# A gated mix of two sequence layers on one Trainium2 core: the order of work inside a chunk of the long convolution, its PSUM ring and its table set-up rearranged

## The chip, the cores and the metric

The kernel runs on one core of a Trainium2 chip (trn2). The metric is device time in microseconds; before the change the median of three runs is 465.64 us (462.01 to 466.97). A separate execution was profiled; it took 465.26 us, and the profile covers a span of 463.5 us of it.

Names of engines, as the profile has them: PE is the matrix engine (PEld its weight loads, which overlap), DVE the vector engine, ACT the scalar engine, POOL and SP the engines that here mostly issue DMAs. A name with a q (SPq, POOLq) is the queue from which an engine issues DMAs. PSUM is the memory that PE writes its sums into, and ACT or DVE must empty a PSUM buffer ("evict" it) before PE can use it again.

## The reference

Two layers read the same `x` (2048 x 1024, bf16) and are mixed by a gate. `A` is a diagonal complex state space layer, `B` a short and a long convolution:

```python
g = sigmoid((x * gate_w).sum(-1, keepdims=True))
# A: h[t] = Lam_bar * h[t-1] + (x @ B_bar.T)[t];  a = 2 Re(h @ C.T) + x * Dskip
# B: a filter of 4 taps on k, times v, then a causal convolution over all 2048 steps
k_shift = sum(k_pad[:, t:t+S] * shift_k[:, ks-1-t] for t in range(4))
kv = k_shift * v
y  = irfft(rfft(kv, 4096) * rfft(ssm_k, 4096))[:2048]     # one filter for each of 1024 channels
b  = x * (y + kv * ssm_D)
return g * a + (1 - g) * b
```

## The kernel before

The kernel has two stages. **The convolution stage** does layer B in eight chunks `c` of 128 channels, roughly the first 255 us. **The scan stage** does layer A after that, with the last of B's results brought in from a scratch buffer in DRAM.

The transform of a chunk is done with matrix products against tables of sines and cosines. The 2048 steps are four blocks of 512; each block is folded about its middle (into a part that is even and one that is odd), transformed to four groups of 128 frequencies, multiplied, and transformed back. The steps of a chunk, with the tile names by which the profile shows them:

- `load` (SP): `kT` (k transposed by the DMA), `kn` (the long filter, transposed) and `v`; three buffers in all.
- `dgs` then `taps`: ACT makes four diagonal matrices `dg` from the identity and the short filter; PE multiplies `kT` by them, 64 matmuls of 128 columns into two PSUM buffers `taps`; ACT evicts them to `ks`.
- `times_v`: DVE multiplies `ks` by `v`; PE reverses the lower half (`mirror`, 2 matmuls); ACT evicts that to `lo`; DVE forms `ev` = `ks` - `lo`, and POOL issues a DMA that adds `lo` into `ks`. A `yield` after the product and one after `lo` let the caller place these three pieces apart.
- `fold_K`: PE folds `kn` (`foldk`, 10 matmuls into two buffers); ACT evicts to `eok`.
- `fwd_K(c, hf)`, `fwd_V(c, hf)`: for half `hf` of the frequencies, PE makes `psk` (16 matmuls) and `psv` (8), two PSUM buffers each; ACT evicts them to `Kh` and `Vh`.
- `products(c, hf)`: DVE multiplies `Kh` by `Vh` block by block and sums into `G`; one of the sums is done by a DMA that POOL issues (`G<-t`, accumulating).
- `inverse(c)`: PE makes `psz` from `G` and the tables `CI`, `SI` (2 x 16 matmuls); ACT evicts to `cv`; SP moves it to DRAM.
- `turn_table(pi)`: not part of B. ACT and DVE make one eighth of the rotation tables `TC`, `TS`, `TCi`, `TSi` of the scan stage (`hr`, `TCS`, `m`, `TCSi`); POOL issues a DMA that adds `m`.

**What sets the order.** All compute goes through the helper `put` (line 99, which is why almost every row of the profile names L99). It ties each instruction to the one before it on the same engine, so on every engine instructions run in the order of the Python code. The generators are advanced by `step` (to the next `yield`) and `run` (to the end), and the loop `for c in range(NC)` is a schedule written out by hand. An iteration `c` handles three chunks at once: with `n = c + 1` and `nn = c + 2`, it makes the transforms of `n`, the products of `c`, the inverse of `c - 1` and the taps and the fold of `nn`. On PE the order of an iteration is

```
psk(n,0)  mirror(n)  psz(c-1)  taps(nn)  psv(n,0)  psk(n,1)  foldk(nn)  psv(n,1)
```

and on ACT `hr`, `Kh` x2, `lo`, `cv` x2, `dg` x4, `ks` x2, `hr`, `TCS` x2, `Vh` x2, `Kh` x2, `eok` x2, `m` x2, `Vh` x2, `TCSi`. In the last two iterations there are no more taps and folds; then `Bu` (`bu`, matmuls of layer A) fills in.

PSUM has room for eight units of 2 KB per partition. Before, the pool `psum` has three buffers of two units, taken in turn by everything above, and `psum1` two single units (`p1`, `p2`) for small things: the columns of parameters at the start, the gate, and the last of the four output tiles at the end.

**The start** (before the loop): the tables `CF`, `SF` of the forward transform and `CI`, `SI` of the inverse are computed from indices (`reduced`, `sincos`, `inverse_angles`, `inverse_table`), the parameters are brought to columns by small matmuls (`psp`), and `state_params` works out the constants of layer A. Chunk 0 takes its own way (`first_times_v`).

**The scan stage**: `Bu(tb, g)` gives 2 x 16 matmuls `bu` for each of 4 blocks of time and 4 groups of states, ACT evicts to `U`, DVE does `scan` (two products and sums, the recurrence as a scan instruction `W`, and again two products and sums, to `hb`), and `Cy` gives 32 matmuls `psy` of each output tile from `hb` and `CT`.

Of the kernel before, what the change touches and what calls it, by code (L numbers as in the profile page):

```python
# [20 lines left out]
def kernel(  # L21
# [57 lines left out]
    psum = pool("psum", 3, space=bass.MemoryType.PSUM)  # L79
    psum1 = pool("psum1", 1, space=bass.MemoryType.PSUM)  # L80
# [9 lines left out]

    def ps1(tag):
        return psum1.tile([128, 512], F32, name=tag, tag=tag)
# [52 lines left out]
    tab_pool = h3pool(h3, "tab", 1)  # L145
    ld = h3pool(h3r, "ld", 3, side="right")
# [11 lines left out]
    prow = rows_[64:96, 0:128]  # L158

    nc.scalar.dma_start(out=skr, in_=B_shift_k.rearrange("(j p) k -> j p k", p=128))  # L160
    pih = consts.tile([128, 1], F32, name="pih")
# [3 lines left out]
    put("act", nc.scalar.activation, out=one, in_=pih, func=ACT.Sin)  # L165
    for i, ap in enumerate((A_Lambda_re, A_Lambda_im, A_log_dt, gate_w)):
        nc.scalar.dma_start(out=prow[i * 8:(i + 1) * 8, :], in_=ap.rearrange("(j p) -> j p", p=128))
# [60 lines left out]
    def sincos(rq, n, sin_out, cos_out, sin_scale):  # L228

        fa = u4([128, n], F32, "fa")  # L230
        act(fa, rq, func=ACT.Abs)
        act(sin_out, rq, func=ACT.Sin, scale=sin_scale)
        act(cos_out, fa, func=ACT.Sin, bias=pih, scale=-TWO_PI)
# [27 lines left out]
    pcol = consts.tile([128, 4 + KS, ND], F32, name="pcol")  # L261
    gwb = consts.tile([128, ND], BF16, name="gwb")
    psp = ps1("p1")[:, 0:32 + ND * KS]
    raise_clock(3)
    for k in range(KS):
        mm(psp[:, 32 + ND * k:32 + ND * (k + 1)], skr[:, :, k], ident[32:32 + ND, 32:32 + ND], True, True)
    raise_clock(6)

    def dgs(c, on_dve=False):
        dg = ks_pool.tile([128, KS, 128], BF16, name="dg", bufs=1)  # L270
        for k in range(KS):
            if on_dve:
                ts(dg[:, k], ident, pcol[:, 4 + k, c:c + 1], None, ALU.mult)
            else:
                act(dg[:, k], ident, func=ACT.Identity, scale=pcol[:, 4 + k, c:c + 1])
        return dg

    hf = u4([128, 2, 512], F32, "h")
    for mt in range(2):
        ts(hf[:, mt], fr_, colm[:, mt:mt + 1], None, ALU.mult)  # L280
    copy(pcol[:, 4:], psp[:, 32:].rearrange("p (i j) -> p i j", j=ND))
# [11 lines left out]
    def inverse_angles(h2):  # L293

        if h2 == 0:
            inv["room"] = xt_pool.tile([128, 2, 2, 512], F32, name="h", tag="xT")
        hi = inv["room"][:, h2]
        for k in range(2):
            fi = 2 * h2 + k
            ts(hi[:, k], trow[0], inv["col"][:, fi:fi + 1], inv["at0"][:, fi:fi + 1], ALU.mult, ALU.add)  # L300
        rq = w4([128, 1024], F32, "rq")
        ts(rq, flat(hi), MAGIC, -MAGIC, ALU.add, ALU.add)
        tt(flat(hi), flat(hi), rq, ALU.subtract)
        return flat(hi)

    def inverse_table(h2, rq):
        sincos(rq, 1024, flat(SI[:, 2 * h2:2 * h2 + 2]), flat(CI[:, 2 * h2:2 * h2 + 2]), -TWO_PI)


    Lre, Lim, logdt = pcol[:, 0], pcol[:, 1], pcol[:, 2]  # L310
# [12 lines left out]
    def state_params():  # L323

        mm(psp[:, 0:32], prow, ident[64:96, 64:96], True, True)
        copy(pcol[:, 0:4], psp[:, 0:32].rearrange("p (i j) -> p i j", j=ND))
        copy(gwb, psp[:, 24:32])
        yield
        dtv = small("dtv")
        act(dtv, logdt, func=ACT.Exp)  # L330
        av = small("av")
        tt(av, dtv, Lre, ALU.mult)
        bv = small("bv")
        tt(bv, dtv, Lim, ALU.mult)
        act(rv, av, func=ACT.Exp)
        ts(thn, bv, 1.0 / TWO_PI, None, ALU.mult)
        yield
        thU = small("thU")
        ts(thU, thn, float(TB), None, ALU.mult)
        frs = []  # L340
        for x, name in ((thn, "th"), (thU, "thU")):
            rq = small(name + "_rq")
            ts(rq, x, MAGIC, -MAGIC, ALU.add, ALU.add)
            fr = small(name + "_fr")
            tt(fr, x, rq, ALU.subtract)
            frs.append(fr)
        sc = []
        for fr, name in zip(frs, ("th", "thU")):
            fa = small(name + "_fa")
            act(fa, fr, func=ACT.Abs)  # L350
            s_ = small(name + "_sin")
            act(s_, fr, func=ACT.Sin, scale=TWO_PI)
            c_ = small(name + "_cos")
            act(c_, fa, func=ACT.Sin, bias=pih, scale=-TWO_PI)
            sc += [s_, c_]
        sth, cth, cs["sU"], cs["cU"] = sc
        yield
        rc = small("rc")
        tt(rc, rv, cth, ALU.mult)
        rs = small("rs")  # L360
        tt(rs, rv, sth, ALU.mult)
        nre = small("nre")
        ts(nre, rc, -1.0, None, ALU.add)
        den = small("den")
        tt(den, Lre, Lre, ALU.mult)
        den2 = small("den2")
        tt(den2, Lim, Lim, ALU.mult)
        tt(den, den, den2, ALU.add)
        invden = small("invden")
        put("dve", V.reciprocal, invden, den)  # L370
        ts(invden, invden, 2.0, None, ALU.mult)
        t_a = small("t_a")
        t_b = small("t_b")
        tt(t_a, nre, Lre, ALU.mult)
        tt(t_b, rs, Lim, ALU.mult)
        tt(t_a, t_a, t_b, ALU.add)
        tt(c2r, t_a, invden, ALU.mult)
        tt(t_a, rs, Lre, ALU.mult)
        tt(t_b, nre, Lim, ALU.mult)
        tt(t_a, t_a, t_b, ALU.subtract)  # L380
        tt(c2i, t_a, invden, ALU.mult)
        ts(mc2i, c2i, -1.0, None, ALU.mult)

    def turn_table(pi, home):
# [6 lines left out]
        ts(rq, h, MAGIC, -MAGIC, ALU.add, ALU.add)  # L391
        tt(rq, h, rq, ALU.subtract)
# [5 lines left out]
        m = home([128, 2, TB], BF16, "m")  # L398
# [121 lines left out]
    def products(c, hf, home=u4):  # L520
# [16 lines left out]
        mult(0, 0, t=at(0))  # L537
        n1 = mult(1, 0, home)
        gather(at(1), n1)
        t2 = mult(0, 1, home)  # L540
# [6 lines left out]
        n1 = mult(2, 0)  # L547
        tt(t2[:, :, 3:], t2[:, :, 3:], n2, ALU.add)
        n3 = mult(3, 0)
# [3 lines left out]
        tt(at(2), at(2), n1, ALU.add)  # L553
        tt(g[:, 0], g[:, 0], t2[:, 1], ALU.subtract)
# [28 lines left out]
    def gate(tb):  # L583
        psg = ps1(f"p{1 + tb % 2}")[:, 0:4]
# [157 lines left out]

    none = iter(())
    dg0 = dgs(0)
    act(flat(SF), rqf, func=ACT.Sin, scale=TWO_PI)
    act(flat(hf), rqf, func=ACT.Abs)
    act(flat(CF), flat(hf), func=ACT.Sin, bias=pih, scale=-TWO_PI)
    act(NSF, SF[:, :, 256:512], func=ACT.Copy, scale=-1.0)
    act(NCF, CF[:, :, 0:256], func=ACT.Copy, scale=-1.0)

    trow[0] = consts.tile([128, TB], mybir.dt.float16, name="row")
    copy(trow[0], iota_i32([128, TB], [[1, TB]], 0, 0, "row"))
    inverse_cols()
    rqi = [inverse_angles(0)]
    sp = state_params()
    first = first_times_v(0, dg0)
    step(first)
    step(sp)
    step(first)
    step(sp)  # L760
    fold = fold_K(0)
    step(fold)
    run(first)
    run(fold)
# [4 lines left out]
    fwd_V(0, 0)  # L769
    fwd_K(0, 0)  # L770
    rqi.append(inverse_angles(1))
    taps(1, dg1)
    p0 = products(0, 0)
    step(p0)
# [3 lines left out]
    fwd_V(0, 1)  # L778
    step(tv)
    run(fold_K(1))  # L780

    for c in range(NC):
        n, nn = c + 1, c + 2
        if n == NC:
            break
        if nn < NC:
            load("kT", nn)
            load("kn", nn)
        if c < 4:
            load_BT(c // 2, c % 2)  # L790
        elif c < 6:
            load_xT(0, halves=(c - 4,))
        else:
            load_xT(1)
            load_BT(2, 0)
            load_BT(2, 1)
        tabs = turn_table(c - 1, u4) if c else none
        back = inverse(c - 1) if c else none
        if c:
            tv = times_v(n)  # L800
            step(tv)
            run(p1)
            step(tabs)
            p0 = products(c, 0)
            step(p0)
        p1 = products(c, 1)
        if nn < NC:
            load("v", nn)

        fwd_K(n, 0)  # L810
        if c:
            step(tv)
            run(tv)
            step(p0)
        else:
            step(p0)
            run(tv)
        run(back)
        if nn < NC:
            dg = dgs(nn)  # L820
        step(tabs)
        step(p1)
# [3 lines left out]
        step(tabs)  # L826
        if c == 0:
            step(sp)
            inverse_table(0, rqi[0])
        fwd_V(n, 0)  # L830
# [3 lines left out]
        fwd_K(n, 1)  # L834
        if nn < NC:
            run(fold_K(nn))
        step(tabs)
        if c == 0:
            inverse_table(1, rqi[1])
        fwd_V(n, 1)  # L840
        run(tabs)
# [3 lines left out]
    with tc.tile_pool(name="fin", bufs=1, side="right") as fin:  # L845
# [11 lines left out]
        run(p1)  # L857
        step(ta)
        step(tb_)
        step(p0)  # L860
        step(ta)
        step(tb_)
        run(back)
# [3 lines left out]
        step(p0)  # L867
        Bu(0, 0)
        step(tb_)
        step(tb_)  # L870
        run(tb_)
        p1 = products(c, 1, room)
        step(p1)
# [63 lines left out]
    for tl in range(3):  # L937
        ps = ps2([128, 2, 512], "psy")
        pss.append(([ps[:, 0], ps[:, 1]], [(slice(0, D), flat(ps))]))
    pa, pb = ps1("p1"), ps1("p2")  # L940
    pss.append(([pa, pb], [(slice(0, 512), pa), (slice(512, D), pb)]))
# [44 lines left out]
```

## Time and profile before

| | us | share of the span |
|---|---|---|
| median of three runs | 465.64 | |
| profiled execution | 465.26 | |
| its span | 463.5 | |
| DVE busy | 404.8 | 87% |
| ACT busy | 255.4 | 55% |
| POOL busy | 61.5 | 13% |
| matmuls `psz`, both tables | 99.6 (256 of them) | |
| matmuls `taps` | 34.5 (512) | |
| DVE idle until `lo` is there | 32.2 (6 times) | |
| DVE idle until the DMA `G<-t` has landed | 6.4 (twice) | |
| DMA `G<-t`, median from issue to landing | 5.4 (4.8 to 9.6) | |

Times in a row of the timeline are: start, duration (of all instructions of the row together), engine, line, operation, output<-inputs, shapes, count, and in brackets the idle time of the engine just before and what ended it. Matmul ends are modelled: a single matmul of 512 columns shows 0.38 us, while in an unbroken row the next one starts 0.2157 us later. So the starts are what to read for how long PE really needs.

### The profile page before, as it was taken

How to read it: one execution, taken by the hardware profiler on the slowest of the kernel's cores; microseconds unless marked ns; L12 is line 12 of the kernel's file. 1: busy time of each engine (PE TensorE's matmuls, PEld its weight loads, DVE VectorE, ACT ScalarE, POOL GpSimd, SP SyncE). 2: the span in 40 equal slices, each digit the busy share in tenths (PEclk: the TensorE clock that was granted, in tenths of full speed). 3: DMA queues.
4: the chain of work that ended last, by engine and by line, in shares of the span. 5: the costliest groups of instructions: out<-in, count | busy, mean ns of one | idle time of the engine just before them, and what ended most of it. 6: DMA issues, size and time to landing. Idle time of an engine off the chain costs nothing.

```text
span 463.5 us, 6282 instructions
## 1 busy us (share of the span) xinstructions
PE 423.8 (91%) x2414; PEld 207.1 (45%) x2414; DVE 404.8 (87%) x571; ACT 255.4 (55%) x311; POOL 61.5 (13%) x80
## 2 busy tenths in 40 slices
PE   7986879888897988985999999999999999999995
PEld 4534335453543536442444454444444444444442
DVE  9798459697896969779968999999999999999973
ACT  7677767859496784957462342523443324557201
POOL 3020101211202121021120000011101011032200
PEclk9999799999999998998899999999999999999999
DMA  8597915957669599968331999224495475379513
GB/s 159 116 181 139 171 45 103 195 114 153 140 133 185 103 190 165 125 134 161 81 63 40 186 184 214 53 45 110 99 197 117 114 163 125 77 164 197 116 24 114
DMA packets 134352, 60.20 MB, mean 130 GB/s; under 512 B 118441, under 2 KB 122545, under 8 KB 134322
## 3 DMA queue, kind: packets, MB, share of 16 engines
q1 hardware_dynamic: 123696, 42.22, 41.1%
q0 software_dynamic: 10544, 17.57, 23.4%
q8 instruction: 19, 0.31, 0.3%
q14 instruction: 11, 0.09, 0.1%
q10 hardware_dynamic: 82, 0.02, 0.0%
HBM read 12.86 MB, written 8.39 MB: 46 GB/s over the span
## 4 chain that ended last, share of the span: by engine, by line
PE 71%; ACT 16%; DVE 7%; issue 5%; POOL 0%; DVEq 0%; ACTq 0%; POOLq 0%
PE bu L99 24%; PE psy L99 21%; PE psz L99 11%; PE taps L99 6%; PE psk L99 4%; ACT Vh L99 4%; PE foldk L99 3%; DVE t L99 3%; ACT Kh L99 2%; ACT dg L99 2%; PE p L99 1%; ACT hr L99 1%; ACT TCS L99 1%; ACT cv L99 1%; ACT m L99 1%
## 5 line engine op out<-in xcount | busy, mean ns | idle before, releaser
L99 PE MATMUL bu<-xT,BT 128*128 128x512 bf16 x512 | 112.3, 379 | 0.0
L99 PE MATMUL psy<-CT,hb 128*128 128x512 bf16 x480 | 105.7, 379 | 0.0
L99 DVE TENSOR_TENSOR t<-Kh,Vh 128x1536 bf16<-128x1536 bf16 (+3 forms) x112 | 82.4, 759 | 0.0
L99 PEld LDWEIGHTS <-BT 128*128 128x128 bf16 x512 | 50.0, 98 | 60.2
L99 PEld LDWEIGHTS <-hb 128*128 128x128 bf16 x512 | 50.0, 98 | 59.9
L99 ACT ACTIVATE U<-bu 128x1024 bf16<-128x1024 f32 x32 | 32.7, 1022 | 52.8 <-PE bu L99 50.4
L99 PE MATMUL psz<-G,CI 128*128 128x512 bf16 x128 | 49.9, 390 | 11.7 <-ACT Kh L99 7.2
L99 DVE TENSOR_TENSOR_SCAN W<-rv,init,A 128x512 bf16<-128x512 f32 x48 | 57.7, 1262 | 0.0
L99 PE MATMUL psz<-G,SI 128*128 128x512 bf16 x128 | 49.7, 389 | 0.0
L99 PE MATMUL taps<-dg,kT 128*128 128x128 bf16 x512 | 34.5, 224 | 9.7 <-ACT dg L99 8.4
L99 DVE TENSOR_TENSOR t<-t 128x1536 bf16<-128x1536 bf16 (+1 forms) x64 | 39.6, 618 | 0.5
L99 PEld LDWEIGHTS <-kT 128*128 128x128 bf16 x512 | 31.6, 101 | 14.7 <-issue 13.7
L99 ACT ACTIVATE cv<-psz 128x1024 bf16<-128x1024 f32 x16 | 16.4, 1023 | 39.1 <-PE psz L99 39.1
L99 DVE TENSOR_TENSOR G<-G,t 128x1024 bf16<-128x1024 bf16 x48 | 31.7, 687 | 7.0 <-DMA G<-t 6.4
L99 PE MATMUL psk<-eok,CF 128*128 128x512 bf16 (+1 forms) x96 | 27.6, 370 | 9.7 <-ACT Vh L99 8.8
L99 ACT ACTIVATE Kh<-psk 128x1024 bf16<-128x1024 f32 x32 | 31.7, 1026 | 5.4 <-PE psk L99 5.4
L99 ACT ACTIVATE ga<-psy,gcols 128x1024 bf16<-128x1024 f32 x8 | 8.9, 1113 | 46.3 <-PE psy L99 46.3
L99 DVE TENSOR_TENSOR ev<-ks,lo 128x1024 bf16<-128x1024 bf16 x7 | 4.8, 691 | 32.2 <-ACT lo L99 32.2
L99 ACT ACTIVATE Vh<-psv 128x1024 bf16<-128x1024 f32 x32 | 30.8, 1014 | 0.9 <-PE psv L99 0.9
L99 POOL DMA_DIRECT2D G<-t x16 | 21.2, 1326 | 71.9 <-DVE t L99 63.4
L99 POOL DMA_DIRECT2D pbb<-gd x12 | 10.3, 860 | 133.3 <-ACT gd L99 68.4
L99 PEld LDWEIGHTS <-CF 128*128 128x128 bf16 x160 | 14.9, 98 | 25.2 <-issue 11.8
(139 smaller groups left out, 593.5 us busy)
## 6 DMA issues: line engine op xcount, KB each, us to landing
G<-t POOLq DMA_DIRECT2D x16, 384.0 KB, 5.4
v<-in_B_v_dram SPq DMA_DIRECT2D x8, 512.0 KB, 5.1
cv_scr<-cv SPq DMA_DIRECT2D x16, 256.0 KB, 2.3
pbb<-cv_scr SPq DMA_DIRECT2D x12, 256.0 KB, 3.2
xr<-in_A_x_dram SPq DMA_DIRECT2D x12, 256.0 KB, 3.5
pbb<-gd POOLq DMA_DIRECT2D x12, 256.0 KB, 3.3
TCSi<-m POOLq DMA_DIRECT2D x8, 256.0 KB, 4.0
ga<-xr POOLq DMA_DIRECT2D x8, 256.0 KB, 3.4
```

The lines of the kernel that those rows point to most:

```text
L99: i = f(*a, **kw)
```

## The change

The parts, with the code cut to its core. One ring of PSUM: four buffers of two units, and everything that used `p1` or `p2` takes one of them.

```diff
-    psum = pool("psum", 3, space=bass.MemoryType.PSUM)
-    psum1 = pool("psum1", 1, space=bass.MemoryType.PSUM)
+    psum = pool("psum", 4, space=bass.MemoryType.PSUM)
...
-    for tl in range(3):
+    for tl in range(4):
         ps = ps2([128, 2, 512], "psy")
         pss.append(([ps[:, 0], ps[:, 1]], [(slice(0, D), flat(ps))]))
-    pa, pb = ps1("p1"), ps1("p2")
-    pss.append(([pa, pb], [(slice(0, 512), pa), (slice(512, D), pb)]))
```

The start: all parameter rows are fetched before the first activation, which is now `Exp` and not `Sin`; the columns for `state_params` are made ahead of the first taps; an absolute value and the negated tables go from ACT to DVE; the inverse angles and tables yield between their pieces.

```diff
-    put("act", nc.scalar.activation, out=one, in_=pih, func=ACT.Sin)
+    put("act", nc.scalar.activation, out=one, in_=pih, func=ACT.Exp)
...
-    act(flat(SF), rqf, func=ACT.Sin, scale=TWO_PI)
-    act(flat(hf), rqf, func=ACT.Abs)
...
-    act(NSF, SF[:, :, 256:512], func=ACT.Copy, scale=-1.0)
-    act(NCF, CF[:, :, 0:256], func=ACT.Copy, scale=-1.0)
+    copy(pcol[:, 0:3], psp[:, 0, 0:3 * ND].rearrange("p (i j) -> p i j", j=ND))
...
+    act(flat(SF), rqf, func=ACT.Sin, scale=TWO_PI)
+    put("dve", V.scalar_tensor_tensor, out=flat(hf), in0=rqf, scalar=-1.0, in1=rqf, op0=ALU.mult, op1=ALU.max)
...
+    ts(NSF, SF[:, :, 256:512], -1.0, None, ALU.mult)
+    ts(NCF, CF[:, :, 0:256], -1.0, None, ALU.mult)
```

`products` is cut into six pieces in place of three, and two sums stand further from what they depend on; `turn_table` yields between its two DVE instructions, and its tile `m` has a pool of its own.

```diff
         mult(0, 0, t=at(0))
+        yield
         n1 = mult(1, 0, home)
         gather(at(1), n1)
+        yield
         t2 = mult(0, 1, home)
...
         n1 = mult(2, 0)
+        n3 = mult(3, 0)
         tt(t2[:, :, 3:], t2[:, :, 3:], n2, ALU.add)
-        n3 = mult(3, 0)
         tt(n1[:, :, 1:], n1[:, :, 1:], n3, ALU.add)
         yield
         g = at(0)
         tt(at(2), at(2), n1, ALU.add)
+        yield
```

The iteration `c` (the loop now ends before the last chunk, `old` is the turn table of the iteration before):

```diff
         if c:
-            tv = times_v(n)
             step(tv)
-            run(p1)
+            step(p1)
             step(tabs)
             p0 = products(c, 0)
             step(p0)
+            run(p1)
+            steps(p0, 2)
+            run(tv)
         p1 = products(c, 1)
...
         fwd_K(n, 0)
...
+        if nn < NC:
+            dg = dgs(nn, c == 0)
+        step(back)
+        step(tabs)
+        step(old)
         run(back)
-        if nn < NC:
-            dg = dgs(nn)
+        run(old)
+        step(p1)
         step(tabs)
+        step(p1)
+        step(p0)
         step(p1)
         run(p0)
         if nn < NC:
             taps(nn, dg)
...
-        fwd_V(n, 0)
+        step(tabs)
+        fwd_K(n, 1)
         step(p1)
...
-        fwd_K(n, 1)
+        fwd_V(n, 0)
         if nn < NC:
             run(fold_K(nn))
+            tv = times_v(nn)
+            step(tv)
...
         fwd_V(n, 1)
-        run(tabs)
+        old = tabs
```

The load of `v` for `nn` moves up beside those of `kT` and `kn`. In the last chunk, the first `Bu` and the products stand between the pieces of the two last turn tables:

```diff
-        run(p1)
+        run(old)
         step(ta)
         step(tb_)
+        Bu(0, 0)
+        step(p1)
+        step(ta)
+        run(p1)
+        step(tb_)
+        step(ta)
         step(p0)
...
-        run(back)
...
+        run(back)
...
-        Bu(0, 0)
```

On PE the order of an iteration is now

```
mirror(n)  psk(n,0)  psz(c-1)  taps(nn)  psk(n,1)  psv(n,0)  foldk(nn)  psv(n,1)
```

and on ACT `lo`, `hr`, `Kh` x2, `dg` x4, `cv`, `m` x2, `cv`, `TCSi`, `ks` x2, `hr`, `TCS` x2, `Kh` x2, `Vh` x2, `eok` x2, `Vh` x2. DVE has the product `ks` by `v` of chunk `nn` at the end of an iteration, ahead of the iteration in which PE mirrors it.

## The prediction

> **What bounds the kernel now.** First the page's busy times and its chain.
>
> ```profile
> PE 423.8 (91%) x2414; PEld 207.1 (45%) x2414; DVE 404.8 (87%) x571; ACT 255.4 (55%) x311; POOL 61.5 (13%) x80
> PE 71%; ACT 16%; DVE 7%; issue 5%; POOL 0%; DVEq 0%; ACTq 0%; POOLq 0%
> ```
>
> PE ends last, but ACT holds 16% of the chain while busy only 55%: PE waits for evictions. The view of who waited for whom, for PE (us in total, times, longest):
>
> ```profile
> PE psk L99 <- ACT Vh L99: 8.8, 8, 4.0
> PE taps L99 <- ACT dg L99: 8.4, 6, 1.4
> PE psz L99 <- ACT Kh L99: 7.2, 6, 1.4
> PE psz L99 <- DVE G L99: 4.5, 1, 4.5
> ```
>
> All of it lies before 219 us. PE's timeline shows one period, taps to taps:
>
> ```profile
> 123.75 4.44 PE L99 MATMUL taps<-dg,kT 128*128 128x128 bf16 x64 [1.40 <-ACT dg L99]
> ...
> 131.86 0.59 PE L99 MATMUL psk<-eok,CF 128*128 128x512 bf16 x2 [0.43 <-ACT Vh L99]
> ...
> 142.39 0.38 PE L99 MATMUL psz<-G,CI 128*128 128x512 bf16 x1 [1.37 <-ACT Kh L99]
> ...
> 150.86 0.22 PE L99 MATMUL taps<-dg,kT 128*128 128x128 bf16 x1 [1.40 <-ACT dg L99]
> ```
>
> 27.11 us, with 3.20 idle. DVE in the same period: a wait for `lo`, and below it rows whose starts tell the price of a dependence.
>
> ```profile
> 144.20 0.69 DVE L99 TENSOR_TENSOR ev<-ks,lo 128x1024 bf16<-128x1024 bf16 x1 [4.07 <-ACT lo L99]
> ...
> 148.69 0.41 DVE L99 TENSOR_TENSOR t<-t 128x512 bf16<-128x512 bf16 x1
> 149.02 0.41 DVE L99 TENSOR_TENSOR t<-Kh,Vh 128x512 bf16<-128x512 bf16 x1
> 149.47 0.43 DVE L99 TENSOR_TENSOR t<-t 128x512 bf16<-128x512 bf16 x1
> 149.81 0.42 DVE L99 TENSOR_SCALAR hr<-hr 128x512 f32<-128x512 f32 x1
> ```
>
> Independent instructions of this size start 0.33 apart (148.69, 149.02); one that needs its predecessor starts 0.45 after it. Last, windows behind three of PE's gaps; the granted clock stands behind POOL's count:
>
> ```profile
> 47.00:53.00 6.00, 5.71 (x16) 2.05 (x16) 4.76 (x6) 3.91 (x5) 1.20 (x1) 0.54 0.88 181
> 177.00:186.00 9.00, 7.81 (x74) 6.27 (x74) 8.93 (x14) 4.77 (x9) 1.20 (x1) 0.81 1.05 152
> 218.00:224.00 6.00, 5.63 (x15) 1.97 (x15) 5.93 (x9) 0.40 (x1) 1.29 (x1) 0.57 0.44 74
> ```
>
> After gaps of 3.95, 1.40 and 4.50 us PE ran at about half clock for some microseconds. From 256 to 440 us it shows no gap and a clock of 1.00.
>
> **A full period after the change.** PE's need, from unbroken stretches: `psk` 3.02 + 3.08, `psv` 1.73 + 1.74, `foldk` 2.24, `mirror` 0.43, `psz` 32 x 0.2157 = 6.90, `taps` 3.58 (18.83 to 22.41, where `dg` was ready). Sum 22.72; against 27.11 that is 3.20 of idle, 0.69 because the first four `taps` were paced by `dg` (128.02 - 123.75 = 4.27), and 0.50 of matmul tails before three waits. Does the new order let PE run so? I put `mirror` at 0 and walk ACT through its order (each eviction 0.90 to 0.92 from start to start, `dg` x4 1.26, `m` x2 1.24, `TCSi` 1.04): `lo` 1.3 to 2.2, `Kh` to 4.6, `dg` to 5.9, `cv` from 7.1 and from 10.6, `TCSi` to 12.5, `ks` to 15.1, `TCS` to 16.8, `Kh` to 18.6, `Vh` to 20.4, `eok` to 22.2, `Vh` to 24.0. `dg` is 4.5 us ahead of the taps at 10.4. With four buffers PE needs the one evicted four earlier; the closest meetings are `foldk` 2 (19.6, free at 18.6), the next `psk` (23.15, its `eok` at 22.2) and its second half (24.7, free at 23.1). No wait, but a cover of only about 1 us. ACT works 19.4 of 22.7.
>
> DVE used 27.11 - 4.07 = 23.04. Setting sums apart removes 0.12 and 0.13 in each of two products and 0.12 in `hr`: 0.62, so 22.42, a cover of 0.3 under PE. Its wait for `lo` goes: `ev` comes 4.9 after the product `ks` by `v`, `lo` 2.2 after the mirror. The product moved past the end of the iteration needs `ks` at 15.1, long before DVE gets there. On POOL, `G<-t` of half 1 is issued near 14.5, behind `TCSi` (12.5), and its sum comes up at 22.4: 7.9 us, where landings took 4.8 to 9.6 (median 5.4). Price between 0 and 1.7 a period; I take 0, by the median. `ks<-lo` is issued near 6, is needed at 17.4, and took 3.3 to 5.7. On SP, `v` moved past a transpose into B's tables is needed 19 us later and took 5.2 at most; the transposes behind it serve later stages.
>
> The Trainium skill ("VectorE: DVE Perf Modes", The DRAIN you can't avoid) says that an instruction starts only once the pipe is empty and that a semaphore costs nothing extra. By it the 0.62 would not come, the period would be DVE's 23.04, and the sum 1.9 larger (six periods of 0.32). The rows above (0.33 against 0.45) speak against it.
>
> **The sum.**
> - *Head, to the taps at 69.53.* From the first `psk` (15.80) PE took 53.73 for 39.84 of issue. New costs: the fold now follows the first mirror, and five DMAs precede the first activation, so that `psk` starts at about 16.3 (+0.5; DVE sets the first mirror at 11.9, not 11.36); and the second inverse table (`fa`, `SI`, `CI`, 0.94 + 0.95 + 1.05) now stands before the last `Vh` of iteration 0, so the second `psk(2,0)` waits some 1.25. An absolute value (1.2, as f32 `rq`), two negations (0.34 each, as `hr`) and `dg` of iteration 0 (0.73, as `dg` at 14.38) go to DVE, in time by the walk; one table load (1.28) leaves ACT. Gain 13.89 - 0.5 - 1.25 - 0.2 of small waits = 11.9.
> - *Four full periods, 69.53 to 177.97:* 4 x 4.39 = 17.6.
> - *Tail, 177.97 to `Bu(0,3)` at 254.49:* PE's issue is taps 3.58, `psk` 3 x 3.05, `psv` 4 x 1.73, `foldk` 2.24, `mirror` 0.43, and 2 `psz` (13.8) and 3 `Bu` (20.7) and `psz(5)` 6.9: 63.7 of 76.52. `Bu(0,0)` now fills the 4.50 wait for `G`; the products need `G` when that ends. Gain 12.8.
> - *From there to the end, 209.0 us:* unchanged. One buffer for the last tile instead of two halves is one DVE instruction of 1.28 for two of 1.40, and nothing else waits there.
>
> The scan stage admits the gain only if DVE brings it too:
>
> ```profile
> 290.62 7.07 PE L99 MATMUL psy<-CT,hb 128*128 128x512 bf16 x32
> ...
> 293.83 1.29 DVE L99 TENSOR_TENSOR hb<-hb,trn 128x1024 bf16<-128x1024 bf16 x2
> ```
>
> The last eight matmuls of this first tile start at 295.80; their `hb` is done at 295.12: 0.7 us of slack. DVE from `ks` by `v` of chunk 7 (ends about 158.7, two ahead of PE) has some 45.0 to its first scan (58.8 before, less waits of 0.78, 4.80, 5.65 and of the dependences). That is 203.7 against 246.84, a gain of 43.1, more than PE's 42.3. So PE's decides.
>
> Span 463.5 - 42.3 = 421.2. Unknown: PE now idles about 2.7 us before the first mirror, and a half clock after it costs 0 to 2.5 (the row behind 47 us); I take 1.2. In iteration 6 the DMAs crowd (share 1.05), where `G<-t` took 9.6: 0 to 2; I take 1.0. 423.4, plus 1.8 outside the span: 425.2. The median stands 0.4 above the profiled run: **425.5 us**, 8.6% less.
>
> The Trainium skill ("TensorE: Matmul & The Clock Gate", What's actually happening) lets the clock halve only after a window of about 3.4 us without work. By it the slow stretch after the gap of 1.40 has another cause and may stay: 1.6 more; and the 2.7 us at the start would cost nothing: 1.2 less. The row at 177 speaks against it, unless what went before counts too.
>
> **Rivals.**
> - *ACT paces PE.* The cover is 1 us, in a fixed order. If each eviction starts 0.1 later than walked (15 in a period), the cover is gone and PE loses about 1.5 to 2 a period, over six 9 to 12: 434 to 438. For: ACT rises from 20.0 of 27.11 to 20.0 of 22.7. Against: `psk` started 0.04 after the eviction it waited for. Chance 0.13.
> - *Gathers pace DVE.* DMA share 0.71 over that period becomes 0.85. If half 1's `G<-t` takes 9.6 everywhere, DVE stands 1.7 a period, and `psz`, which meets its `G` 1.4 after DVE finishes it, waits with it: 22.42 + 1.7 = 24.1, six times 1.4 = 8.4: 434. Chance 0.11.
> - *Slower than before.* The same place: `G<-t` behind `TCSi` on POOL, the sum on DVE, then `psz`. To eat 42 in six periods it must cost 7 each: a landing of 7.9 + 0.3 + 7 = 15.2 us and more; at 17 the time is 478. Longest seen 9.6, at a share of 1.05. Chance 0.03.
> - *No difference:* the chain moves to DVE. Its work, 404.8, plus 2.6 moved to it, less 5.0 (8 x 0.62), and its 0.9 at the start and 8 at the end leave a floor near 411, so it cannot hold 465 without new waits of 50. That the edit does less than it says is excluded: the built order of each engine is the one walked. Chance 0.03.
>
> **The numbers.** Forecast as walked (419 to 431) 0.66; ACT 0.13; gathers 0.11; slower 0.03; none 0.03; something between 438 and 460, 0.04. The range runs from 420 (no allowances, less the spread of the runs before, 3.6 below their median) to 439. About 1% is what a measurement tells from no change: faster 0.93, within 0.04, slower 0.03.
>
> **What would show it.** The taps should follow each other every 22.7 us with no `dg` wait; `ev<-lo` should vanish from DVE's waits; the gap before `psz` at the last chunk should be filled with `bu`; no clock near 0.55 after 20 us. A wait `psk <- ACT` of 0.3 or more a period would show the first rival, `G <- DMA G<-t` the second; a period above 24 makes the prediction wrong.

## The result, and the profile after

The kernel after takes 429.87 us, the median of four runs (428.22 to 433.98), beside 463.82 for the kernel before: a ratio of 0.928 (95% interval 0.918 to 0.938). Run again later, on the chip of the last experiments, it took 427.44 (six runs, 425.11 to 430.00) beside 465.29: 0.919 (0.915 to 0.923). The forecast was 425.5, in a range of 420 to 439. The profiled execution took 431.18, with a span of 429.4. Ratios here leave out executions more than 1.5% longer than the fastest of their kernel: 439.18 and 439.41 of a_ring3, 440.77 of a_spread, 440.24 of a_xT_late.

The busy times on the page of the kernel after:

```profile
PE 411.8 (96%) x2375; PEld 205.0 (48%) x2413; DVE 403.3 (94%) x577; ACT 249.1 (58%) x303; POOL 61.5 (14%) x80
```

The chain of this profile can be followed back only to 154.23, so its shares can't be set beside those of before. In the later profile (after_again) the chain goes back to the start:

```profile
PE 44%; DVE 42%; DMA 7%; issue 4%; ACT 2%; DVEq 0%; ACTq 0%
```

ACT has gone from 16% of the chain to 2%, and PE from 71% to 44%. DVE, with about the work of before (403.3 beside 404.8), now holds nearly as much of the chain as PE, and DMAs appear in it: the two engines run almost evenly, and some of what delays them is a transfer. The view of who waited for whom, for PE (us in total, times, longest):

```profile
PE psz L95 <- DVE G L95: 2.3, 5, 1.4
PE mirror L95 <- DVE ks L95: 1.8, 2, 1.3
PE psv L95 <- ACT Kh L95: 1.6, 1, 1.6
PE psv L95 <- DMA ks<-lo: 1.5, 1, 1.5
...
PE psk L95 <- ACT Vh L95: 1.2, 1, 1.2
```

and for DVE:

```profile
DVE G L95 <- DMA G<-t: 8.8, 3, 4.1
...
DVE ev L95 <- ACT lo L95: 1.6, 1, 1.6
```

The wait `taps <- ACT dg` (8.4 before) is gone, and so are all but one of the waits of `psk` for `Vh`; DVE's wait for `lo` fell from 32.2 to 1.6. DVE's wait for the accumulating DMA `G<-t` (the gather) is not new: it was 6.4 in two waits, and is 8.8 in three here and 5.6 in three in the later profile. But one of the three, of 2.65 at 95.59, now lies in a period. PE's timeline, one period:

```profile
128.45 3.74 PE L95 MATMUL taps<-dg,kT 128*128 128x128 bf16 x64
...
151.12 3.74 PE L95 MATMUL taps<-dg,kT 128*128 128x128 bf16 x64
```

22.67 us, no idle time at either, and the taps take 3.74 where they took 4.44. Three of the four periods are 22.67; the third, after the wait at 95.59, is 23.38, with the mirror waiting 0.53 for DVE's `ks` at 118.08.

The span falls into four stretches at events that every kernel here has: the taps of chunk 3, the taps of chunk 7 (four periods later) and the first matmul of `Bu(0,3)`, read from PE's timeline. The table has the forecast's walk (without its 2.2 of allowances) and all kernels of the experiments below.

| kernel | to taps 3 | four periods | tail to `Bu(0,3)` | from there |
|---|---|---|---|---|
| before | 69.53 | 108.44 | 76.52 | 209.0 |
| forecast | 57.63 | 90.88 | 63.7 | 209.0 |
| after | 59.73 | 91.39 | 68.87 | 209.4 |
| after, again (after_again) | 57.90 | 91.01 | 66.01 | 209.4 |
| before + ring (b_ring4) | 66.82 | 103.01 | 77.22 | 208.7 |
| before + early `dg` (b_dg_early) | 69.60 | 99.40 | 73.84 | 208.9 |
| before + both (b_ring4_dg) | 63.50 | 91.08 | 75.82 | 208.7 |
| before + both + early `Bu` (b_three) | 65.31 | 91.08 | 68.95 | 209.4 |
| after, three buffers (a_ring3) | 64.10 | 92.24 | 71.62 | 209.7 |
| after, late `dg` (a_dg_late) | 60.08 | 104.62 | 66.91 | 209.4 |
| after, late `Bu` (a_bu_late) | 59.20 | 91.67 | 75.00 | 208.8 |
| after, transposes moved (a_spread) | 60.38 | 90.69 | 73.37 | 208.8 |
| after, xT moved (a_xT_late) | 58.58 | 90.69 | 69.37 | 209.0 |
| after, moved clear (best3) | 58.99 | 91.61 | 66.70 | 209.4 |
| the same, table late (best4) | 58.39 | 92.25 | 65.22 | 209.4 |

Of the 34.1 us between the spans of before and after, 9.8 came from the start, 17.1 from the four periods and 7.6 from the tail; the scan stage gave back 0.4.

### The profile page after: what moved, and what is told of

Same layout as the page of the kernel before. It is cut to its first block, busy times and chain, and to the rows that moved or that the text cites. A ratio compares the mean times of both kernels' runs of the same rounds, so it can differ in the third digit from the quotient of the medians.

```text
span 429.4 us, 6238 instructions
## 1 busy us (share of the span) xinstructions
PE 411.8 (96%) x2375; PEld 205.0 (48%) x2413; DVE 403.3 (94%) x577; ACT 249.1 (58%) x303; POOL 61.5 (14%) x80
## 4 chain that ended last, share of the span: by engine, by line
DVE 30%; PE 24%; DMA 5%; issue 4%; ACT 1%; DVEq 0%; ACTq 0%
PE psy L95 17%; DVE W L95 9%; PE bu L95 6%; DVE t L95 5%; DVE trn L95 4%; DVE A L95 4%; DVE hb L95 4%; DMA G<-t 3%; DVE G L95 2%; DMA TCSi<-m 2%; DVE hr L95 1%; DVE BT L95 0%; DVE xr L95 0%; PE p L95 0%; ACT TCSi L95 0%
## 5 line engine op out<-in xcount | busy, mean ns | idle before, releaser
L95 PE MATMUL psy<-CT,hb 128*128 128x512 bf16 x502 | 111.8, 379 | 0.9 <-DVE hb L95 0.3
L95 PE MATMUL psz<-G,CI 128*128 128x512 bf16 x128 | 48.5, 379 | 1.7 <-DVE G L95 1.6
L95 PE MATMUL psz<-G,SI 128*128 128x512 bf16 x128 | 48.5, 379 | 0.7 <-DVE G L95 0.7
L95 DVE TENSOR_TENSOR t<-t 128x1536 bf16<-128x1536 bf16 (+1 forms) x64 | 38.1, 615 | 0.0
L95 PE MATMUL taps<-dg,kT 128*128 128x128 bf16 x512 | 31.8, 225 | 0.0
L95 POOL DMA_DIRECT2D pbb<-gd x12 | 10.3, 860 | 125.9 <-ACT gd L95 114.0
L95 ACT ACTIVATE BT<-psy,gcols 128x1024 bf16<-128x1024 f32 x6 | 6.7, 1109 | 30.9 <-PE psy L95 30.9
L95 PE MATMUL psk<-eok,SF 128*128 128x512 bf16 (+1 forms) x95 | 24.0, 361 | 0.4
L95 PEld LDWEIGHTS <-SF 128*128 128x128 bf16 x160 | 15.6, 98 | 17.2 <-issue 2.0
```

The lines of the kernel that those rows point to most:

```text
L95: i = f(*a, **kw)
```

## The experiments

### Single parts added to the kernel before

**b_ring4**: only the ring of four (with it the last output tile, as in the change).

```diff
-    psum = pool("psum", 3, space=bass.MemoryType.PSUM)
-    psum1 = pool("psum1", 1, space=bass.MemoryType.PSUM)
+    psum = pool("psum", 4, space=bass.MemoryType.PSUM)
...
-        return psum1.tile([128, 512], F32, name=tag, tag=tag)
+        return ps2([128, 2, 512], tag)[:, 0]
```

> The kernel before with one ring of four PSUM tiles and nothing else of the change. Theory (the prediction's terms are separate and add up): in each period the waits psk <- ACT Vh (0.43) and psz <- ACT Kh (1.37) go and with them some 0.3 of matmul tails, 2.1 in all, while the taps still wait for dg (1.40) and are paced by it (0.69): a period of 25.0 against 27.11, six periods 12.7, so about 451 us. Rival (dg is the real pace, the ring only a symptom): the late dg of ACT takes over what the ring gave, the wait taps <- ACT dg grows from 1.4 to about 3 in each period and the time stays at 462 to 466.

457.31 us (454.67 to 457.65) beside 465.42, a ratio of 0.981 (0.976 to 0.987): between the two expectations. The waits for `Vh` and `Kh` inside the period are gone, as the first said, and `dg` is waited for no longer than before (1.40). But the taps follow each other after 26.57, 24.94, 26.56 and 24.94 us: every second period has what was expected, the others 1.63 more. In these the taps take 6.07 us and not 4.44. Windows of b_ring4 (from and to, length, then busy time and count for PE, PEld, DVE, ACT, POOL, then PE's granted clock, DMA share, GB/s):

```profile
65.17:68.59 3.42, 1.80 (x21) 1.18 (x19) 3.35 (x8) 2.19 (x5) 0.00 (x0) 1.00 0.46 120
68.59:72.00 3.41, 3.41 (x35) 3.41 (x33) 3.41 (x4) 1.02 (x1) 1.19 (x1) 0.50 0.00 0
92.48:95.89 3.41, 2.28 (x33) 1.92 (x33) 3.34 (x8) 1.73 (x5) 0.00 (x0) 1.00 0.43 117
95.89:99.31 3.42, 3.37 (x42) 2.55 (x41) 3.38 (x5) 2.47 (x4) 1.20 (x1) 1.00 0.04 8
116.37:119.79 3.42, 1.80 (x17) 1.04 (x16) 3.35 (x9) 2.19 (x5) 0.00 (x0) 1.00 0.78 207
119.79:123.20 3.41, 3.41 (x36) 3.41 (x34) 3.41 (x4) 1.02 (x1) 0.66 (x1) 0.50 0.02 5
```

The half clock behind these gaps lasts 3.41 us each time, and its starts at 68.59 and 119.79 lie 51.20 apart, 15 x 3.413: a fixed grid. The same gap of 1.40 fell wholly into one cell of it before 68.59 and before 119.79 (PE idle for 1.62 of 3.42) and across a cell's edge near 92.48 (1.13 idle), and only the cells after the first two are slow. So the price of a wait depended here on where in the grid it fell.

**b_dg_early**: only `dg` ahead of the inverse stage.

```diff
-        run(back)
         if nn < NC:
             dg = dgs(nn)
+        run(back)
```

> The kernel before with the four dg tables written ahead of the inverse product's stage instead of behind it, nothing else of the change. Theory: the wait taps <- ACT dg (1.40) and its pacing (0.69) go, a period of 25.0, six periods 12.5: about 451 us. Rival: the three PSUM tiles are the pace; ACT's evictions are put behind dg by 1.26 us, psk <- ACT Vh and psz <- ACT Kh grow by 1 to 2 us a period and the time stays within 1% of 464.

453.13 us (452.69 to 455.52), 0.975 (0.969 to 0.980). The theory held: `taps <- ACT dg` is left once (in the start), all four periods are 24.85, and the waits `psk <- ACT Vh` (0.43) and `psz <- ACT Kh` (1.37) did not grow at all.

**b_ring4_dg**: both.

The edits are the two above.

> The kernel before with both edits, the ring of four and the early dg, but mirror, products, sums and B's products where they were. Theory: PE keeps no wait of its own in a period, so the period falls to DVE's 23.04, six periods 24, about 440 us; what is left to the kernel after (430) is the head, the tail's gap and the sums. Rival: the mirror's place is what counts; DVE still waits 2 us and more a period for lo, the period stays at 25 or above and the time at 450 or above.

441.28 us (440.76 to 442.47), 0.948 (0.944 to 0.953). The time is the expected one, but not by the expected way. The periods are 22.67, 22.67, 22.79 and 22.95, and DVE waits for `lo` only once, in the first iteration. DVE's own step, read where it has no idle time, in b_ring4_dg:

```profile
76.68 1.22 DVE L98 TENSOR_TENSOR ks<-ks,v 128x2048 bf16<-128x2048 bf16 x1
...
99.65 1.22 DVE L98 TENSOR_TENSOR ks<-ks,v 128x2048 bf16<-128x2048 bf16 x1
...
122.61 1.22 DVE L98 TENSOR_TENSOR ks<-ks,v 128x2048 bf16<-128x2048 bf16 x1
```

22.97 and 22.96 (23.04 had been reckoned), more than PE's 22.67. PE drew on the lead that DVE had from the start, and only the last two periods show DVE's pace. The mirror, which here stands where it stood before, costs nothing in the period once PE is fast.

**b_three**: both, and the first product of B ahead of the inverse stage in the last chunk.

```diff
         step(ta)
         step(tb_)
+        Bu(0, 0)
         step(p0)
...
         step(p0)
-        Bu(0, 0)
         step(tb_)
```

> The kernel before with three edits: the ring of four, the early dg, and the first product of B ahead of the inverse stage in the last chunk; products, mirror, sums and inverse tables as before. Theory (the three edits carry nearly all of the change): against the two edits alone (441) another 5 to 6 us go, the wait psz <- DVE G of 6.0 disappears, about 435; what remains for all other edits is 3 to 5 us, most of it before the fourth taps. Rival (B's product early is only worth something with the products' new order, since DVE is late): the time stays at 440 or more.

436.53 us (436.32 to 439.62), 0.940 (0.935 to 0.944). The tail fell by 6.9 (75.82 to 68.95), as the theory had it, though a wait `psz <- DVE G` of 1.7 stayed. What all other edits are worth was put too low: 9.1 between this median and the 427.44 of the kernel after in the same group. The two profiled executions are 10.4 apart; by the table 7.4 of that lies before taps 3, and 2.9 in the tail. Waits before taps 3 that b_three has and the kernel after does not: 1.40 for `dg` at 35.83, with half clock behind it (6.06 us of taps instead of 3.74), 2.44 of `foldk` for `Vh`, 1.2 of `psk` for `eok`, 0.87 of `mirror` for `Vh`. The edits of the start were not run one by one, so which of them removes which wait is not shown.

### Single parts taken from the kernel after

**a_ring3**: three buffers of two units and two halves again.

```diff
-    psum = pool("psum", 4, space=bass.MemoryType.PSUM)
+    psum = pool("psum", 3, space=bass.MemoryType.PSUM)
+    psum1 = pool("psum1", 1, space=bass.MemoryType.PSUM)
```

> The kernel after with PSUM divided as before, a ring of three and two single halves, nothing else. In the kernel before, the ring of four alone took away all waits of psk and psz for ACT. Theory (in the new order ACT is early enough by itself): three tiles nearly suffice, the taps still follow each other every 22.7 to 23.1 us and the time rises by 0 to 3 us, to 432 to 435 beside a before of 465. Rival (the ring is the main thing in any order): psk <- ACT and psz <- ACT return with 1.5 to 2 us a period, a period of 24.5, and the time rises by 10 us to 442.

A ratio of 0.929 (0.922 to 0.937) to before, from the runs of 431.09 and 433.91, near the theory's 432 to 435. The times alone don't decide, with two further runs of 439.18 and 439.41; the period does. The profile is of the execution of 439.41, and even there three of four periods are 22.82, 0.15 longer than with four buffers, and not the rival's 24.5. It shows another price, in the start: `psk <- ACT Vh` at 52 is 2.69 (1.17 with four) and half clock follows. The gather issued at 160.4 takes 12.6 in it. Whether the ring of three makes such long executions more frequent (two of four here, none of ten of the kernel after) is open.

**a_dg_late**: `dg` of the full periods behind the inverse stage.

```diff
-        if nn < NC:
-            dg = dgs(nn, c == 0)
+        if nn < NC and c == 0:
+            dg = dgs(nn, True)
         step(back)
...
         run(back)
+        if nn < NC and c:
+            dg = dgs(nn)
         run(old)
```

> The kernel after with the dg tables of the full periods written behind the inverse stage again, as before, nothing else. Theory: the taps wait 1.4 for dg in each of five periods and are paced by it (0.69), period 24.8, or 26.4 where the idle time falls into one window of 3.4 us and the granted clock halves in the next one; 10 to 15 us in all, 441 to 447 beside a before of 465. Rival (in the new order something else, DVE, paces the period and hides it): the period stays below 23.3 and the time within 2 us of 432.

443.23 us (442.80 to 444.85), 0.953 (0.948 to 0.958). The theory held to the period: the taps at 60.08, 86.64, 113.20, 138.14 and 164.70 are 26.56, 26.56, 24.94 and 26.56 apart. The windows of a_dg_late before and after 88.5 show the same grid at work:

```profile
85.10:88.50 3.40, 1.78 (x22) 1.28 (x21) 3.40 (x6) 3.22 (x6) 0.00 (x0) 0.99 0.20 77
88.50:91.90 3.40, 3.40 (x36) 3.40 (x34) 3.40 (x7) 1.02 (x1) 2.07 (x2) 0.51 0.53 89
```

1.62 idle, then 3.4 us at half clock.

**a_bu_late**: the first product of B back behind the inverse stage of the last chunk.

```diff
         step(tb_)
-        Bu(0, 0)
         step(p1)
...
         run(tb_)
         step(p0)
+        Bu(0, 0)
```

> The kernel after with the first product of B (Bu(0,0)) put back behind the inverse stage of the last chunk, nothing else. Theory (it fills PE's wait for G there): PE stands 4.5 to 6.5 us before psz of chunk 6, Bu(0,3) begins that much later and the time rises by 4.5 to 7 us, to 436 to 439 beside a before of 465. Rival (DVE and its gathers set the tail, so that it makes no difference where PE does B's products): Bu(0,3) begins within 1 us of 220 and the time stays at 432.

435.95 us (434.39 to 440.14), 0.938 (0.931 to 0.945). As the theory had it, `Bu(0,3)` begins 5.9 later than in the first profile of the kernel after, at 225.87; the tail is 75.00, beside 68.87 and 66.01 in the two profiles. PE's wait in a_bu_late is longer than that:

```profile
PE psz L95 <- DVE G L95: 7.8, 1, 7.8
```

and the clock stands at half from 185.0 to 195.2.

### The tail

The first profile had a tail of 68.87 where 63.7 had been walked. Its events, on POOL, SP, DVE, PE and ACT of the kernel after:

```profile
154.23 1.53 POOL L95 DMA_DIRECT2D G<-t  x1
```

```profile
152.74 7.03 SPq L95 DMA_TRANSPOSE xT<-in_A_x_dram  x2
159.81 6.78 SPq L95 DMA_TRANSPOSE BT<-in_A_B_re_dram  x1
```

```profile
161.48 1.22 DVE L95 TENSOR_TENSOR ks<-ks,v 128x2048 bf16<-128x2048 bf16 x1
166.82 0.69 DVE L95 TENSOR_TENSOR G<-G,t 128x1024 bf16<-128x1024 bf16 x1 [4.13 <-DMA G<-t]
...
190.15 0.69 DVE L95 TENSOR_TENSOR G<-G,t 128x1024 bf16<-128x1024 bf16 x1 [2.04 <-DMA G<-t]
```

```profile
169.31 0.38 PE L95 MATMUL psz<-G,CI 128*128 128x512 bf16 x1 [1.39 <-DVE G L95]
...
182.23 0.59 PE L95 MATMUL psv<-ev,CF 128*128 128x512 bf16 x2 [1.59 <-ACT Kh L95]
```

```profile
179.51 0.63 ACT L95 ACTIVATE hr<-hr 128x512 f32<-128x512 f32 x1 [1.52 <-DVE hr L95]
```

The DMA of 154.23 lands 12.5 us later (DVE starts at once, at 166.82), while transposes of x and B are in flight. DVE loses 4.13, `psz` waits 1.39 for it; DVE is then late with `hr`, ACT waits 1.52 for that at 179.5 with `Kh` queued behind, and `psv` waits 1.59 for `Kh`. The theory was that the transposes lengthen `G<-t`. Three kernels moved them.

**a_spread**: all of the tail's transposes later.

```diff
-            load_xT(1)
-            load_BT(2, 0)
-            load_BT(2, 1)
...
         run(back)
+        if c == 6:
+            load_BT(2, 0)
+            load_BT(2, 1)
         run(old)
...
-        load_BT(3, 0)
-        load_BT(3, 1)
...
         run(back)
+        load_BT(3, 0)
+        load_BT(3, 1)
+        load_xT(1)
```

> The kernel after with the transposes of B's third group moved behind the inverse stage in iteration 6, and those of the fourth group and the second x tile behind the same stage of the last chunk, nothing else. Theory (DMA crowd in the tail is what the prediction missed): G<-t, which took 12.5 us there, lands in 5 to 9, DVE's two waits of 4.1 and 2.0 for it shrink to below 1 each, psz's wait of 1.4 and psv's of 1.6 go, and the time falls by 4 to 6 us to 424 to 426. Rival (the gather is late for another reason, its place on POOL or its own bytes): the landing stays above 10 us, the waits stay and the time stays at 429 to 431. A second rival: the moved transposes arrive too late for Bu and the time rises by 2 us or more.

0.930 (0.922 to 0.938), from runs of 431.28 to 435.12: no gain, and 424 to 426 had been expected. The wait at 167 is gone, but in its place DVE waits 4.29 at 189.43, where B's third group is now fetched, and 3.71 at 214.94, where x and the fourth are; PE's clock halves at 193.0 and 216.9.

**a_xT_late**: only the x tile moved.

```diff
-            load_xT(1)
             load_BT(2, 0)
...
         run(back)
+        load_xT(1)
         step(tb_)
```

> The kernel after with the second x tile's transposes (two) moved from the start of iteration 6 to behind the inverse stage of the last chunk, B's transposes where they were. Theory (transposes in flight lengthen the accumulating gathers): the first G<-t of the tail, issued near 154 and landing after 12.5, now lands in 6 to 9, DVE's wait at 167 falls from 4.1 to below 1, psz's wait of 1.39 goes, the gathers near 197 and 207 become longer by 1 to 3 and are covered; Bu(0,3) begins at 216 to 219 instead of 220 and the time falls by 1 to 4 us. Rival (the gather is slow for another reason, such as its place behind TCSi on POOL): it lands after 11 or more and nothing changes.

0.928 (0.921 to 0.935), from runs of 429.46 to 432.26: no gain either. The first gather's wait is gone in this profile too, and this time the second gather, issued at 176.52 beside B's fourth group, lands after 11.4 and costs 4.16. The tail is 69.37.

**best3**: x's second tile fetched between the two halves of the last inverse stage, B's fourth group behind the inverse stage before it. **best4**: besides, the second inverse table behind the last `Vh` of iteration 0.

```diff
-        load_BT(3, 0)
-        load_BT(3, 1)
...
         run(back)
+        load_BT(3, 0)
+        load_BT(3, 1)
...
-        run(inverse(c))
+        back = inverse(c)
+        step(back)
+        load_xT(1)
+        run(back)
```

> The kernel after with the tail's transposes kept out of the way of the accumulating gathers: the second x tile's moved between the two halves of the last inverse stage, B's fourth group behind the inverse stage of chunk 6, B's third group where it was. Theory (transposes in flight lengthen G<-t, and where they were moved so far the long gather moved with them): the gathers issued near 154 and 177 both land in 5 to 8, DVE's waits for G<-t in the tail fall from 6 or 8 to below 2, no half clock follows, Bu(0,3) begins 64 to 66 after the last taps instead of 69, and the time is 3 to 5 us below the kernel after: a ratio of 0.917 to 0.922 to before, 427 to 429. Rival (the tail has too many bytes for any order): another gather takes 10 or more, near 196 or 206, and the time stays at that of after, 431 to 432.

```diff
-        if c == 0:
-            run(turns)
         fwd_V(n, 1)
+        if c == 0:
+            run(turns)
```

> The kernel of the run before this one with the second inverse table (fa, SI, CI on ACT) moved behind the last eviction of Vh in iteration 0. Theory: psk's wait of 1.17 at 51 goes, psz then waits some 0.6 for CI, so the taps at 59.7 come 0.5 earlier and the time falls by 0.5. Rival: lo and the evictions behind the table come later, another wait takes its place (psz for ACT or DVE for lo), no gain or a loss of up to 1 us.

**after_again**: the kernel after, unchanged.

> The kernel after once more, unchanged, for comparison on the same chip. Theory: a ratio of 0.925 to 0.931 to before, so 431 to 433; its profile shows the gather of the tail at over 10 us again (theory: a fixed collision with the transposes), or (rival: chance of that one execution) at less than 8.

best3 426.72 us (425.42 to 428.52), 0.918 (0.914 to 0.921); best4 426.83 (424.58 to 427.80), 0.917 (0.913 to 0.920); the unchanged kernel 427.44 (425.11 to 430.00), 0.919 (0.915 to 0.923). The three intervals lie on each other: no version that beats the kernel after was found, and best3's time alone would have looked like the theory's success. Its profile does not show that success: the gather issued at 153.7 landed after 10.3, where 5 to 8 was expected, though DVE's waits for gathers in the tail were small (1.94 and 1.37). The unchanged kernel came out below the 431 to 433 expected of it, and its profile, of an execution of 426.10, says why nothing was gained. Its waits for DVE:

```profile
DVE G L95 <- DMA G<-t: 5.6, 3, 2.4
```

and DVE's only row of the tail with such a wait:

```profile
185.09 0.69 DVE L95 TENSOR_TENSOR G<-G,t 128x1024 bf16<-128x1024 bf16 x1 [2.36 <-DMA G<-t]
```

Beside the same transposes the first gather of the tail came in time here, and the longest landing of all sixteen is 9.6. So the 12.5 of the first profile is not a fixed collision, and the last expectation's theory fell; its rival held as to that gather. The long gathers named here all lie beside transposes, but the same program had one of 12.5 in one execution and none in another. Over the five profiles with the transposes where the kernel after has them, that gather took 12.5, 8.2, 12.6 (a_ring3), 12.3 (a_dg_late) and 6.8 (a_bu_late); over the four with x's moved, 6.5, 6.7, 10.3 and 8.3. The second set is lower on the whole, but the two overlap, so how much the transposes do is left open. In best4 `psk`'s wait of 1.17 is gone from PE's waits, but the start is not shorter for sure (58.39 beside 59.73 and 57.90), and a gain of half a microsecond can't be told in these intervals.

## Why the prediction was right, point by point

**The mechanism was the one forecast.** PE was bound by ACT's evictions and `dg`, and the new order lets it run unbroken until DVE and the gathers come near. The period was walked as 22.72 and is 22.67, with no `dg` wait and no PSUM wait. The cover of about 1 us for ACT, on which the first rival stood, held in both profiles of the kernel after: PE has no wait for an eviction in the four periods.

**DVE's terms.** Walked as 23.04 without and 22.42 with the sums set apart; measured 22.96 (b_ring4_dg) and 22.34: the reckoned 0.62 in full. DVE in the kernel after:

```profile
116.80 1.22 DVE L95 TENSOR_TENSOR ks<-ks,v 128x2048 bf16<-128x2048 bf16 x1
...
139.14 1.22 DVE L95 TENSOR_TENSOR ks<-ks,v 128x2048 bf16<-128x2048 bf16 x1
...
149.70 0.42 DVE L95 TENSOR_TENSOR t<-Kh,Vh 128x512 bf16<-128x512 bf16 x1
150.04 0.75 DVE L95 TENSOR_TENSOR t<-t 128x512 bf16<-128x512 bf16 x2
150.71 0.42 DVE L95 TENSOR_SCALAR hr<-hr 128x512 f32<-128x512 f32 x1
```

The four instructions at the end of a product that started 0.33, 0.45 and 0.34 apart now start 0.34 apart throughout (149.70, 150.04, and 0.67 for the next two). The prediction worked out from the Trainium skill ("VectorE: DVE Perf Modes", The DRAIN you can't avoid) that this saving would not come, and there it read only half: the same paragraph adds that "A next op that is not held starts earlier". The rows (0.34 against 0.45) bear out that there are such earlier starts. The worth of the saving is small all the same: without it DVE falls behind PE by 0.3 a period, and only after its lead is used up.

**The clock.** After the gap of 1.3 us ahead of the first mirror the clock stayed at 1.00 in the kernel after, so the 1.2 set aside for it was not needed, and the slow stretch after the gap of 1.40 went with the gap. The page "TensorE: Matmul & The Clock Gate" of the Trainium skill (What's actually happening) has a free-running window of 3413 ns; the starts of half clock 15 x 3.413 apart agree with it. The page has the clock halve after an idle window of about 3.4 us; here the window was not idle throughout, and 1.62 us of idle time in 3.41 were enough.

**The tail was mis-sized.** The step that failed is the last allowance: "In iteration 6 the DMAs crowd (share 1.05), where `G<-t` took 9.6: 0 to 2; I take 1.0." The tail measured 5.2 above the walk in the first profile and 2.3 in the second. The price was taken as a wait of DVE alone, bounded by the longest landing of one profile. A landing of 12.5 came, and the wait ran on through `hr` on ACT and `Kh` to `psv`: of the 5.2, 1.9 lie in the first `psz`, 1.8 in `psv`, and 1.4 in the two later `psz`, which meet `G` just as DVE finishes it. These two make 1.7 of the 2.3 in the second profile, so part of what was missed does not hang on the landing of 12.5. The second rival (gathers pace DVE) had the right place but not the right extent: in the period, single gathers cost DVE 2 to 3 us, which its lead absorbed all but 0.3 to 0.7; and PE met the rest at the mirror, which waits for `ks`, not at `psz`.

**The start.** Walked to 57.63; 59.73 and 57.90. The wait of the second `psk` was forecast at 1.25 and is 1.17 (0.84 in the second profile). Not forecast was `psv`'s wait for the DMA `ks<-lo` at 42.76, 1.54 in one profile and none in the other.

**The sum for the two profiles.** For the first, 2.1 in the start, 0.5 in the periods, 5.2 in the tail and 0.4 behind it, less the 2.2 of allowances, is 6.0: 429.4 against 423.4. For the second, 0.3, 0.1, 2.3 and 0.4 less 2.2 is 0.9: 424.3. That the sum came so near is in part luck: the 1.2 set aside for a half clock that did not come stood in for waits in the tail that had not been forecast. The medians fell by 34.0 and 37.9, where 40.1 had been forecast.

**What the prediction did not see** is that two parts do the same thing. In the period the ring of four (old order, 22.67) and the new order (three buffers, 22.82) each take away the 2.0 to 2.2 us of PSUM waits that b_dg_early still has (24.85); with both, one is spare there. The early `dg` has no such substitute: without it, and with the ring of four, the period is 24.94 or 26.56 in the old order as in the new.

## What to carry to other kernels

When an engine waits in turn for two things, price the parts of a change also with the others absent: here a gain of 17 us in the periods needed only two short edits, and one of them, the ring of four, removes the same waits as the new order does. A gap in PE's work costs its own length and in some places a stretch at half clock behind it; here the gap of 1.40 cost 3.0 where that stretch followed. And where a stall hangs on a DMA's landing, take two profiles of the unchanged kernel before moving anything: the difference between them was as large as the effect looked for.

## What the runs showed of the hardware that was not expected

In these profiles the granted clock changes in cells of 3.41 us on a grid that is fixed within an execution. Of the cells at full clock, those with an idle time of PE up to 1.5 us were followed by full clock, those from 2.25 up by half clock in the whole next cell; between, both occurred (half after 1.62 in b_ring4, full after 1.60 in the kernel before; in a_spread full after 1.95 at 39.4 and half after 1.95 at 189.6), so the idle time alone does not decide there. A cell at half clock was followed by another when PE idled 1.19 in it (192.7 in b_ring4_dg). A fixed wait of 1.40 therefore cost 1.63 more in some periods than in others, and in b_ring4, whose periods are no multiple of the cell, the two alternate.

The runs of the kernel before in the last group mostly go with their mean granted clock: 462.48 at 0.986, 464.24 at 0.983, 465.29 at 0.980, 467.20 at 0.977; one of the eleven breaks the order, 463.62 at 0.988. One cell at half clock is 3.41 x 0.5 / 464, 0.0037 of the mean clock, so the first and the last of the four differ by two to three such cells; that the place of the grid differs from run to run was not tested.
